# Sums of weights all formed in the second batch, seven products per block from the third batch on

## The chip, the core and the metric

The kernel runs on one core of a Trainium2 chip. The metric is the device time of one execution in microseconds (us), the median of several executions. The engines are named as in the profile: PE is TensorE (matmuls), PEld its weight loads, DVE is VectorE, ACT is ScalarE, POOL is GpSimd, SP is SyncE, which here issues transfers only.

## The reference

There are eight batches. In each, attention with eight heads (576 positions, head size 64, a window of 128 earlier positions, a linear bias by distance) gives 576 rows of 512 numbers. They then go through a bilinear feed-forward layer.

```python
scores = scale * np.matmul(q, k.transpose(0, 1, 3, 2))
mask = (rel >= 0) & (rel < window)
scores = np.where(mask, scores + bias[None], -1000000000.0)
attn = softmax(scores)                      # written out in the reference
attn_out = np.matmul(attn, v)
x = attn_out.transpose(0, 2, 1, 3).reshape(B * S, H * D)      # 4608 x 512
a, b = x @ w_a, x @ w_b                                       # 512 x 1536 each
return (a * b) @ w_out                                        # 1536 x 512
```

## The kernel before

All numbers are kept as pairs of 16-bit halves (a high part and a rest), so one product of two matrices takes three matmuls: high by high, high by rest, rest by high. The 1536 hidden columns are cut into 12 blocks `f`, the 576 rows of a batch into two halves of 288, the 512 inputs into chunks of 128.

**Stages.** PE's order is written out by hand: `batch(b)` weaves the feed-forward work of batch b with the attention of later batches, which `Pace` spreads evenly over it. So each batch has an *up* stage (both first products of the layer, all 12 blocks) and a *down* stage (the last product, tiles `dn_ps`, L952), and between these matmuls stand the attention's: scores `sc_ps` (L384), row norms `qtot` (L337), probabilities times values `x_ps` (L507). I call the stages by batch: the second batch is the first that `batch` handles (b = 1); the first batch has its own functions.

**Two ways for a block.** `up_plain` computes the four quarter results of a block (two row halves by a and b) as eight half products, 48 matmuls of 128x128 by 128x288. `up_fast` gets them from seven (Winograd's scheme), 42 matmuls, and needs sums: of the inputs (further slots of `xs`, made in `split_x` from the attention's output, some of them by POOL at L455, L458, L460, L465), and of the weights (`wsum`, and slot 3 of `wup` written over). In `up_fast` four of the seven products pass through one tile `ch` in turn, and ACT, DVE and POOL read and combine them as they come (L881 to L916). `ways[b]` says which blocks of batch b go which way: the second batch is all plain, the third has six plain blocks and six fast ones, the fourth two and ten, and from the fifth on all are fast.

**Steps that form sums of weights.** `sums_of_weights` has 24 steps, two for each block. A step is five POOL operations (L248 on 128x512, L249 to L252 on 128x128), and one step later two ACT copies (L258) and two DVE subtractions (L260) that split the sums into halves. The 16 steps of blocks 0 to 7 keep their interim sums in a part of `wsum` that is not yet in use; those of blocks 8 to 11 (`ws`) take two buffers each of the pool `t`, whose four buffers also hold the attention's exponentials. `quota[b]` says how many steps run beside the up stage and the down stage of batch b, and between which of its pieces: an entry `(a, z, steps)`. A twenty-fifth call only finishes the last step.

**What sets the other engines' order.** For ACT, DVE and POOL a scheduler puts the instructions of this program in the order in which its own clock has them ready, with some marked urgent; on the chip each engine then takes them strictly in that order. `issue_after` holds an instruction behind another in that clock.

Of the kernel before, what the change touches and what calls it, by code (L numbers as in the profile page):

```python
# [21 lines left out]
B, H, S, D = 8, 8, 576, 64  # L22
# [24 lines left out]
def attention_then_bilinear_ffn(ctx: ExitStack, tc: tile.TileContext, qT, kT, vP, w_a, w_b, w_out, rel, slopes2, outT):  # L47
# [221 lines left out]
    def load_v(b):  # L269

        st = State()
        st.v = work.tile([P, NPAIR, VCOLS], F32, tag="v", name="v")
        sp.dma_start(st.v, vP[b])
        st.xq = work.tile([P, S], BF16, tag="xq", name="xq")
        return st
# [93 lines left out]
    def scores(o, bi):  # L369

        ps = ps_at.tile([P, 512], F32, tag="at", name="sc_ps")
        t = work.tile([P, 512], F32, tag="t", name="t", bufs=4)
        for i, c in BANKS[bi]:
            w = TILES[i][1]
            qq, kk = slice(64 * i, 64 * i + 64), slice(64 * i + 64 - w, 64 * i + 64)
            if o.b == 1:
                with tc.issue_after(last_pv[0].ins):
                    for e in range(2):
                        r = slice(64 * e, 64 * e + 64)
                        pe.matmul(ps[r, c:c + w], o.q[r, qq], o.k[r, kk], start=True, stop=True)  # L380
                continue
            for ks, last in ((o.kh, False), (o.kl, True)):
                for e in range(2):
                    pe.matmul(ps[64 * e:64 * e + 64, c:c + w], o.qs[:, e, qq], ks[:, e, kk], start=not last, stop=last)  # L384
        for i, c in BANKS[bi]:
            pc, w = TILES[i]
            n = o.n
            vec.tensor_tensor_reduce(out=t[:, c:c + w], in0=ps[:, c:c + w], in1=o.bias[:, WIN - w:WIN], scale=-0.125 if o.b == 1 else o.neg, scalar=3.0e38, op0=ALU.add, op1=ALU.min, accum_out=o.mn[:, n:n + 1])  # L388
            act.activation(t[:, c:c + w], t[:, c:c + w], AF.Exp, bias=o.mn[:, n:n + 1], scale=-1.0, accum_out=o.sm[:, n:n + 1])  # L389
            o.parts.append((n, t[:, c:c + w], pc, w))  # L390
            o.n += 1
# [48 lines left out]
    def split(n, src):  # L440
        act.copy(xs[:, n, 0, :, :], src)  # L441
        vec.tensor_tensor(out=xs[:, n, 1, :, :], in0=src, in1=xs[:, n, 0, :, :], op=ALU.subtract)  # L442

    def split_x(st, plain, fast):

        b11, b12, b21, b22 = (st.v[:, k:k + 2, t:t + HT] for k in (0, 2) for t in (0, HT))
        split(0, b11)
        if plain:
            split(1, b21)
            split(2, b22)  # L450
            split(B12, b12)
        if not fast:
            return
        yield
        pool.tensor_tensor(out=b11, in0=b12, in1=b11, op=ALU.subtract)  # L455
        if not plain:
            split(2, b22)
        pool.tensor_tensor(out=b12, in0=b22, in1=b12, op=ALU.subtract)  # L458
        split(4, b11)
        pool.tensor_tensor(out=b22, in0=b22, in1=b11, op=ALU.subtract)  # L460
        yield
        if not plain:
            split(1, b21)
        split(6, b12)
        pool.tensor_tensor(out=b21, in0=b21, in1=b22, op=ALU.subtract)  # L465
        yield
        split(5, b22)
        split(3, b21)
        yield
# [197 lines left out]
    def attention():  # L667
# [16 lines left out]
        def split(o):  # L684
            if o and o.b > 1:
                split_qk(o)
# [10 lines left out]
        st, prev = load_v(1), None  # L697
# [4 lines left out]
        for i in range(n + 1):  # L702
            b, p = 1 + i // NPAIR, i % NPAIR

            two = 2 if o and o.b >= 2 else 1
            for bi in range(two if o else 0):
                scores(o, bi)
            with behind():
                nxt = squares(i + 1)
            if p == 1 and b > 1:  # L710
                st = load_v(b)
            if p == (1 if b == 1 else 2):
                v_scale(st)
            yield i + 1 / 7
            if o and two == 1:
                scores(o, 1)

            if p == 2:

                with tc.issue_after(first_reads[0].ins) if first_reads[0] else ExitStack():  # L720
                    late.vhl = split_v(st, late.p)
            elif prev and p != 1:
                prev.vhl = split_v(st, prev.p)
            yield i + 2 / 7
            if p == 2:
                pv(late.p, st, late, late.vhl)
                transpose_probs(prev)
                split(nxt)
            if o and p != 2:
                with behind():  # L730
                    normalize(o)
            if p != 2:
                split(nxt)
            yield i + 3 / 7
            if o:
                scores(o, 2)
            if prev and p not in (1, 2):
                pv(prev.p, st, prev, prev.vhl)
            if two == 2 and p in (1, 3):
                if p == 2:  # L740
                    with behind():
                        normalize(o)
                scores(o, 3)
            yield i + 4 / 7
            if p == 2:
                prev.vhl = split_v(st, prev.p)
                if two == 1 or p not in (1, 3):
                    with behind():
                        normalize(o)
            if o and (two == 1 or p not in (1, 3)):  # L750
                scores(o, 3)
            lay_out(nxt)
            load(i + 2)
            if p == (0 if b == 1 else 1):
                v_squares(st, (0, 1))
            if prev and p == 0:
                states[b - 1] = st
                assert started["down"] == b - 2
                for k, _ in enumerate(split_x(st, b - 1 <= 3, b - 1 >= 2)):
                    yield i + (4.2 + 0.2 * k) / 7  # L760
            yield i + 5 / 7
            if o:
                with behind():
                    normalize(o)
            if p == (0 if b == 1 else 1):
                v_squares(st, (2, 3))
            yield i + 6 / 7
            if prev and p == 0:
                hidden_scale(st)
            if p == 2:  # L770
                pv(prev.p, st, prev, prev.vhl)
            if p == 1:
                late = prev
            elif o:
                transpose_probs(o)
            prev, o = o, nxt
            yield i + 1
# [232 lines left out]


    every = list(range(NF))
    ways = [(every, [])] * 2 + [(every[6:], every[:6]), (every[10:], every[:10])] + [([], every)] * (B - 4)
    att = Pace(attention())
    spread = sums_of_weights()

    quota = [((), ()), (((8, 48, 9),), ((0, 48, 4),)), (((0, 24, 3),), ((0, 48, 5),)), ((), ((0, 48, 4),))] + [((), ())] * (B - 4)

    def first_batch():
        st = states[0]  # L1020
# [60 lines left out]
```

## Time and profile before

| | |
|---|---|
| Time, median of 3 executions | 991.28 us (991.03 to 994.67) |
| The profiled execution | 989.81 us, span of its instructions 988.0 us |
| PE, DVE, ACT, POOL busy in the span | 962.1, 669.0, 635.6, 255.3 us |
| Matmuls | 9339 in the record |
| Second batch | up 200.3 to 281.8 us, down to 324.1 |
| Third batch | up to 400.0 us, down to 441.1 |
| Fourth batch | up to 513.2 us, down to 554.8 |

The stage bounds are where PE's first matmul of the next kind starts (L952 for down, L856 for up). All times are from the start of the span. A row of the trace's timeline reads: start, duration, engine, line, operation, output <- inputs, shape, count, and in brackets the idle time of that engine just before, with what ended it.

### The profile page before, as it was taken

What the parts mean: (1) busy time and instruction counts of PE and PEld (TensorE: products, weight loads), DVE (VectorE), ACT (ScalarE), POOL (GpSimd) and SP (SyncE); (2) the same over time, 40 slices, a digit from 0 to 9 for tenths busy, and PEclk for the clock granted to TensorE, in tenths of its full rate; (3) what the DMA queues carried; (4) which work ended last, traced back from release to release, by engine and by line L of the source; (5) the groups of instructions that cost most, each with busy time, mean ns of one, the idle gap of its engine ahead of it and who ended that gap; (6) DMA issues with size and microseconds to landing.
All of it is one profiled execution on the core that took longest, in us unless ns stands there. A gap on an engine that the chain in (4) does not pass through costs nothing.

```text
span 988.0 us, 23867 instructions
## 1 busy us (share of the span) xinstructions
PE 962.1 (97%) x9339; PEld 748.9 (76%) x9339; DVE 669.0 (68%) x1867; ACT 635.6 (64%) x1729; POOL 255.3 (26%) x309
## 2 busy tenths in 40 slices
PE   7899999999999999999999999999999999999998
PEld 5567777677777777777777777777777777877776
DVE  5979998668688657777778677757776576514520
ACT  5977769667676667766767766777667766413321
POOL 1211122032546313541225222211232012311100
PEclk8999999999999999999999999999999999999999
DMA  8434753664337234463345362373245432200001
GB/s 333 168 126 172 231 154 67 151 158 92 80 74 183 68 69 87 107 172 75 68 92 121 120 118 65 87 191 84 59 84 117 133 74 38 55 34 5 1 13 36
DMA packets 148432, 102.82 MB, mean 104 GB/s; under 512 B 120032, under 2 KB 128352, under 8 KB 147296
## 3 DMA queue, kind: packets, MB, share of 16 engines
q1 hardware_dynamic: 138816, 91.77, 38.2%
q10 hardware_dynamic: 9504, 9.54, 3.0%
q8 instruction: 73, 1.20, 0.5%
q14 instruction: 39, 0.32, 0.1%
HBM read 48.33 MB, written 9.44 MB: 58 GB/s over the span
## 4 chain that ended last, share of the span: by engine, by line
PE 69%; DVE 12%; ACT 7%; DMA 7%; issue 3%; POOL 1%; SPq 0%; ACTq 0%; DVEq 0%
PE ch L856 19%; PE dn_ps L952 18%; PE p L856 14%; PE up_ps L856 9%; PE x_ps L507 4%; DMA v<-in_vP 4%; PE sc_ps L384 3%; DVE phl L406 2%; PE dn_ps L818 2%; ACT t L389 1%; DVE wsum L135 1%; DVE xs L442 1%; ACT phl L405 1%; DVE wsum L134 1%; DMA qk<-in_kT 1%
## 5 line engine op out<-in xcount | busy, mean ns | idle before, releaser
L856 PEld LDWEIGHTS <-wup 128*128 128x128 f16 x3072 | 296.3, 98 | 82.0 <-issue 5.7
L952 PE MATMUL dn_ps<-h,wdn 128*128 128x288 f16 x2016 | 254.4, 286 | 0.0
L952 PEld LDWEIGHTS <-wdn 128*128 128x128 f16 x2016 | 193.9, 98 | 52.0 <-issue 0.2
L856 PE MATMUL up_ps<-xs,wup 128*128 128x288 f16 x1536 | 194.6, 286 | 1.1 <-ACT rc L867 0.8
L856 PEld LDWEIGHTS <-wsum 128*128 128x128 f16 x1152 | 111.7, 98 | 32.0 <-issue 2.5
L911 POOL TENSOR_TENSOR rc<-rc,row 128x288 f32<-128x288 f32 x64 | 62.3, 974 | 279.8 <-DVE row L909 263.9
L389 ACT ACTIVATE t<-t,mn 128x192 f32<-128x192 f32 (+2 forms) x252 | 107.2, 427 | 24.5 <-DVE mn L388 24.4
L856 PE MATMUL ch<-xs,wup 128*128 128x288 f16 x768 | 115.0, 286 | 0.5 <-ACT row L893 0.5
L856 PE MATMUL p<-xs,wup 128*128 128x288 f16 x768 | 115.1, 286 | 0.0
L406 DVE SCALAR_TENSOR_TENSOR phl<-t,rin,phl 128x192 f16<-128x192 f32 (+2 forms) x252 | 104.6, 454 | 15.3 <-ACT phl L405 15.1
L856 PE MATMUL ch<-xs,wsum 128*128 128x288 f16 x768 | 111.5, 286 | 1.1 <-ACT rc L881 1.1
L848 ACT CAST h<-rc 128x576 f16<-128x576 f32 x96 | 64.1, 668 | 69.1 <-DVE rc L916 37.2
L405 ACT ACTIVATE phl<-t,rin 128x192 f16<-128x192 f32 (+2 forms) x252 | 88.9, 425 | 25.3 <-DMA pT<-phl 12.7
L849 DVE TENSOR_TENSOR h<-rc,h 128x576 f16<-128x576 f32 x90 | 69.5, 772 | 30.5 <-ACT h L848 29.7
L388 DVE CUSTOM_DVE_ANT_0 t<-sc_ps,bias,neg 128x192 f32<-128x192 f32 (+2 forms) x216 | 73.9, 389 | 7.6 <-PE sc_ps L384 7.5
L957 ACT ACTIVATE row<-dn_ps,oi 128x288 f32<-128x288 f32 x56 | 27.6, 493 | 55.9 <-PE dn_ps L952 55.9
L893 ACT ACTIVATE row<-ch,g 128x288 f32<-128x288 f32 x64 | 31.8, 497 | 48.9 <-PE ch L856 48.9
L442 DVE TENSOR_TENSOR xs<-v,xs 128x576 f16<-128x576 f32 x52 | 47.8, 935 | 21.4 <-ACT xs L441 21.3
L888 DVE TENSOR_TENSOR rc<-p,rc 128x288 f32<-128x288 f32 x64 | 29.1, 454 | 44.3 <-PE p L856 34.7
L365 POOL TENSOR_SCALAR bias<-rel_sb,ninv,sl_sb 128x192 f32<-128x192 f32 x24 | 20.0, 832 | 147.8 <-DVE mn L388 129.8
L856 PE MATMUL p<-xs,wsum 128*128 128x288 f16 x384 | 57.5, 286 | 0.0
L436 POOL TENSOR_TENSOR xq<-xq,sq 128x576 bf16<-128x576 bf16 x22 | 29.2, 1325 | 75.7 <-ACT sq L435 75.7
(155 smaller groups left out, 1386.1 us busy)
## 6 DMA issues: line engine op xcount, KB each, us to landing
v<-in_vP SPq DMA_DIRECT2D x8, 1280.0 KB, 6.2
out<-row ACTq DMA_DIRECT2D x62, 144.0 KB, 1.8
qk<-in_qT SPq DMA_DIRECT2D x28, 288.0 KB, 4.0
qk<-in_kT SPq DMA_DIRECT2D x28, 288.0 KB, 4.4
wdn<-in_w_a SPq DMA_DIRECT2D x12, 512.0 KB, 5.1
wdn<-in_w_b SPq DMA_DIRECT2D x12, 512.0 KB, 6.1
wdn<-in_w_out SPq DMA_DIRECT2D x12, 512.0 KB, 4.6
qst<-qkh SPq DMA_DIRECT2D x24, 144.0 KB, 2.7
```

The source lines that it names most:

```text
L388: vec.tensor_tensor_reduce(out=t[:, c:c + w], in0=ps[:, c:c + w], in1=o.bias[:, WIN - w:WIN], scale=-0.125 if o.b == 1 else o.neg, scalar= ...
L389: act.activation(t[:, c:c + w], t[:, c:c + w], AF.Exp, bias=o.mn[:, n:n + 1], scale=-1.0, accum_out=o.sm[:, n:n + 1])
L405: act.activation(phl[:, 0, pc:pc + w], e, AF.Copy, scale=s)
L406: vec.scalar_tensor_tensor(out=phl[:, 1, pc:pc + w], in0=e, scalar=s, in1=phl[:, 0, pc:pc + w], op0=ALU.mult, op1=ALU.subtract)
L442: vec.tensor_tensor(out=xs[:, n, 1, :, :], in0=src, in1=xs[:, n, 0, :, :], op=ALU.subtract)
L507: last = pe.matmul(xp[oc // 512][64 * h:64 * h + 64, o0:o0 + w], vt[0:rows, c:c + 64], probs(pt, rows, blocks, h), start=(n == 0 and first ...
L848: act.copy(h[:, f, :, 0, :], hid)
L849: eng.tensor_tensor(out=h[:, f, :, 1, :], in0=hid, in1=h[:, f, :, 0, :], op=ALU.subtract)
L856: pe.matmul(ps[:, 0:HT], w[:, wi, k, :], xs[:, b, xi, k, :], start=(first and n == 0), stop=(last and n == len(ks) - 1), skip_group_check= ...
L893: last_read[0] = last_main[0] = act.activation(mid, ch, AF.Copy, scale=st.g)
L911: pool.tensor_tensor(out=x0, in0=x0, in1=mid, op=ALU.mult)
L952: pe.matmul(ps[:, 0:HT], wdn[:, f, wi, e * P:(e + 1) * P], h[:, f, t, hi, :], start=(m == 0 and n == 0), stop=(m == NF - 1 and n == 2))
```

## The change

Two tables and one condition change. All 24 steps (and the finishing call) run in the second batch, 15 beside its up stage and 10 beside its down stage; before, it was 13 there, 8 in the third batch, 4 in the fourth. The third and fourth batch use `up_fast` for all 12 blocks. And `split_x` no longer makes slot B12 of `xs` for these two, so it makes seven splits (L441 on ACT, L442 on DVE) in place of eight, in the order that the fifth batch already has.

```diff
-                for k, _ in enumerate(split_x(st, b - 1 <= 3, b - 1 >= 2)):
+                for k, _ in enumerate(split_x(st, b - 1 <= 1, b - 1 >= 2)):
...
-    ways = [(every, [])] * 2 + [(every[6:], every[:6]), (every[10:], every[:10])] + [([], every)] * (B - 4)
+    ways = [(every, [])] * 2 + [([], every)] * (B - 2)
...
-    quota = [((), ()), (((8, 48, 9),), ((0, 48, 4),)), (((0, 24, 3),), ((0, 48, 5),)), ((), ((0, 48, 4),))] + [((), ())] * (B - 4)
+    quota = [((), ()), (((4, 48, 15),), ((0, 48, 10),))] + [((), ())] * (B - 2)
```

PE's order is the same as before in every stage but the up stages of the third and fourth batch, and these two now read row for row like that of the fifth. There 36 and 12 matmuls go. On the other engines the order changes from the second batch's up stage on.

POOL at the end of the second batch's up stage, up to the first sum of inputs for the third (L455). Before:

```order
L252 TENSOR_TENSOR wsum<-wsum 128x128
L249 TENSOR_TENSOR wsum<-wsum 128x128
L252 TENSOR_TENSOR wsum<-wsum 128x128
L250 TENSOR_TENSOR wsum<-wsum 128x128
L251 TENSOR_TENSOR wsum<-wsum 128x128
L252 TENSOR_TENSOR wsum<-wsum 128x128
L455 TENSOR_TENSOR v<-v 128x2x288
L458 TENSOR_TENSOR v<-v 128x2x288
L436 TENSOR_TENSOR xq<-xq,sq 128x576
L365 TENSOR_SCALAR bias<-rel_sb,ninv,sl_sb 128x192
L248 TENSOR_TENSOR wsum<-wup 128x512 x2
L460 TENSOR_TENSOR v<-v 128x2x288
```

Now, at the same place:

```order
L249 TENSOR_TENSOR wsum<-wsum 128x128
L252 TENSOR_TENSOR wsum<-wsum 128x128
L248 TENSOR_TENSOR wsum<-wup 128x512
L250 TENSOR_TENSOR wsum<-wsum 128x128
L251 TENSOR_TENSOR wsum<-wsum 128x128
L249 TENSOR_TENSOR wsum<-wsum 128x128
L252 TENSOR_TENSOR wsum<-wsum 128x128
L250 TENSOR_TENSOR wsum<-wsum 128x128
L251 TENSOR_TENSOR wsum<-wsum 128x128
L455 TENSOR_TENSOR v<-v 128x2x288
L252 TENSOR_TENSOR wsum<-wsum 128x128
L248 TENSOR_TENSOR ws_4275<-wup 128x512
```

Since the last bias (L365) POOL now has four steps instead of three ahead of L455, all but the fourth's L252, and behind it come steps of the last four blocks.

ACT at the same place, where the split of that sum (the last L441 here) stands ahead of the last hidden block's copy (L848). Before:

```order
L867 COPY rc<-up_ps 128x288
L258 CAST wup<-wsum 128x128
L258 CAST wsum<-wsum 128x3x128
L441 CAST xs<-v 128x576 x2
L848 CAST h<-rc 128x2x288
L389 ACTIVATE t,sm<-t,mn 128x64
```

Now:

```order
L867 COPY rc<-up_ps 128x288
L258 CAST wup<-wsum 128x128
L258 CAST wsum<-wsum 128x3x128
L258 CAST wup<-wsum 128x128
L258 CAST wsum<-wsum 128x3x128
L441 CAST xs<-v 128x576
L848 CAST h<-rc 128x2x288
L389 ACTIVATE t,sm<-t,mn 128x64
```

One more pair of copies stands in front, and the split that waits for L455 is still ahead of L848.

DVE in the second half of that batch's down stage, around `both` (L329), for which PE's `qtot` waits. Before:

```order
L388 ISA t,mn<-sc_ps,bias,neg 128x192
L388 ISA mn 128x1
L329 TENSOR_SCALAR both<-halves,qs 128x2
L442 TENSOR_TENSOR xs<-v,xs 128x576
L402 RECIPROCAL rin<-rin 128x5
```

Now:

```order
L442 TENSOR_TENSOR xs<-v,xs 128x576
L964 TENSOR_SCALAR oi<-g,smin,so 128x1
L965 TENSOR_SCALAR oi<-oi,sv 128x1
L966 RECIPROCAL oi<-oi 128x1
L329 TENSOR_SCALAR both<-halves,qs 128x2
L260 TENSOR_TENSOR wup<-ws_4488,wup 128x128
L260 TENSOR_TENSOR wsum<-ws_4424,wsum 128x3x128
L388 ISA t,mn<-sc_ps,bias,neg 128x64
```

`both` has moved ahead of the scores' operations (L388), and between it and them stand subtractions of the steps.

## The prediction

> **What bounds the kernel now.** I read the page first: busy times, granted clock, and the chain that ended last.
>
> ```profile
> PE 962.1 (97%) x9339; PEld 748.9 (76%) x9339; DVE 669.0 (68%) x1867; ACT 635.6 (64%) x1729; POOL 255.3 (26%) x309
> ...
> PEclk8999999999999999999999999999999999999999
> ...
> PE 69%; DVE 12%; ACT 7%; DMA 7%; issue 3%; POOL 1%; SPq 0%; ACTq 0%; DVEq 0%
> ```
>
> PE is busy 97% of the span at full clock, and the chain lies on it for 69%. So a matmul that goes is worth its time, and an operation elsewhere costs nothing until PE waits for it. Second view: busy time by stage, cut where PE goes from up to down and back. The rows are up and down of the second, third, fourth, fifth and sixth batch in turn.
>
> ```profile
> core 0: us, PE busy (x) PEld busy (x) DVE busy (x) ACT busy (x) POOL busy (x), PEclk, DMA share, GB/s
> 200.30:281.80 81.50, 80.25 (x799) 63.27 (x798) 61.10 (x176) 59.44 (x172) 38.11 (x56) 1.00 0.47 105
> 281.80:324.10 42.30, 41.13 (x409) 31.89 (x408) 33.18 (x98) 30.36 (x90) 20.74 (x23) 1.00 0.61 146
> 324.10:400.00 75.90, 74.96 (x747) 59.16 (x745) 52.54 (x144) 50.88 (x136) 18.57 (x25) 1.00 0.30 65
> 400.00:441.10 41.10, 40.86 (x408) 31.83 (x406) 30.98 (x96) 29.34 (x88) 21.32 (x27) 1.00 0.67 159
> 441.10:513.20 72.10, 71.89 (x723) 56.78 (x721) 52.17 (x146) 50.90 (x137) 17.57 (x19) 1.00 0.37 76
> 513.20:554.80 41.60, 40.87 (x409) 31.81 (x406) 30.58 (x96) 29.51 (x89) 19.04 (x22) 1.00 0.60 150
> 554.80:626.40 71.60, 71.14 (x711) 55.58 (x709) 52.58 (x149) 50.71 (x135) 16.31 (x16) 1.00 0.37 75
> 626.40:667.10 40.70, 40.70 (x408) 31.91 (x407) 25.45 (x93) 29.05 (x87) 8.72 (x7) 1.00 0.62 157
> 667.10:737.80 70.70, 70.70 (x710) 55.51 (x708) 50.78 (x144) 48.85 (x130) 16.32 (x16) 1.00 0.35 73
> 737.80:778.60 40.80, 40.80 (x409) 31.97 (x408) 24.56 (x90) 27.77 (x83) 8.71 (x7) 1.00 0.67 153
> ```
>
> The fifth and sixth batch are what the third and fourth are to become: all blocks by seven products, no steps beside them. DVE's column shows what the steps cost beside PE: in a down stage it is busy 33.2, 31.0 and 30.6 us with them, 25.5 and 24.6 without.
>
> **The gain.** 36 matmuls go from the third batch and 12 from the fourth. In a run of fast products, six matmuls follow the six before them in 0.74 us:
>
> ```profile
> 561.72 0.90 PE L856 MATMUL p<-xs,wup 128*128 128x288 f16 x6
> 562.46 0.90 PE L856 MATMUL ch<-xs,wsum 128*128 128x288 f16 x6
> ```
>
> So 48 of them are 48 x 0.74 / 6 = 5.9 us. By stages instead: PE's order there becomes that of the fifth batch, so I put the mean of the fifth and sixth in their place. Up: 71.15, against 75.90 and 72.10, saves 4.75 and 0.95. Down: 40.75, against 41.10 and 41.60, saves 0.35 and 0.85. Together 6.9 us, of which about 1.0 are waits that go with the steps. I take 6.9; the bounds are 5.9 (the waits stay) and 7.6 (5.9, and PE's whole idle time of the four stages, 2.1 us, falls to the 0.46 of the fifth and sixth batch's means). The split of slot B12 that both batches save (one L441, one L442 each) lies beside PE and counts nothing.
>
> **What the moved steps take.** Twelve calls move into the second batch: six more beside its up stage (9 to 15), six more beside its down stage (4 to 10, the last of which only finishes). One step, by the rows of the `ws` tiles:
>
> ```profile
> L248 POOL TENSOR_TENSOR ws<-wup x8: 1145/1152/1266, 402.2 to 545.8; 128x512 f32<-128x512 f16 x8
> ...
> L252 POOL TENSOR_TENSOR ws<-ws,ws x8: 453/457/652, 405.4 to 553.1; 128x128 f32<-128x128 f32 x8
> L258 ACT CAST wup<-ws x8: 283/286/298, 417.3 to 556.8; 128x128 f16<-128x128 f32 x8
> L258 ACT CAST wsum<-ws x8: 509/512/522, 417.5 to 557.0; 128x384 f16<-128x384 f32 x8
> L260 DVE TENSOR_TENSOR wup<-ws,wup x8: 279/292/743, 417.6 to 557.1; 128x128 f16<-128x128 f32 x8
> L260 DVE TENSOR_TENSOR wsum<-ws,wsum x8: 545/558/1755, 418.2 to 557.5; 128x384 f16<-128x384 f32 x8
> ```
>
> POOL takes 1.15 + 4 x 0.457 = 2.98 us, ACT 0.80, DVE 0.85. DVE's part is dearer than that while POOL works. These are DVE's groups of the second batch's down stage (four steps' subtractions), then one of the fifth's (none):
>
> ```profile
> L406 DVE SCALAR_TENSOR_TENSOR phl<-t,rin,phl 128x192 f16<-128x192 f32 x10 | 6.6, 701 | 0.5 <-ACT phl L405 0.5
> L260 DVE TENSOR_TENSOR wsum<-wsum 128x384 f16<-128x384 f32 x4 | 4.2, 1044 | 0.0
> L260 DVE TENSOR_TENSOR wup<-wsum,wup 128x128 f16<-128x128 f32 x4 | 3.2, 807 | 1.0 <-ACT wup L258 1.0
> L406 DVE SCALAR_TENSOR_TENSOR phl<-t,rin,phl 128x192 f16<-128x192 f32 x13 | 4.7, 413 | 0.6 <-ACT phl L405 0.6
> ```
>
> The same L406 takes 701 ns beside POOL's steps and 413 without; the two L260 take 1.85 us there, not 0.85. So a step costs DVE 0.85 to 1.85 us. The Trainium skill states the reason (SBUF — State Buffer, Who interferes with whom): a VectorE instruction with two SBUF inputs and a GpSimd instruction that reads SBUF exclude each other for the whole instruction, whichever issues first. The trace agrees that they delay each other, by 0.29 us for an L406 on average; how far the exclusion goes decides the second rival.
>
> **What it costs, place by place in the second batch.** PE's order is unchanged there, so each cost is a wait of PE.
>
> *Up stage.* ACT goes from 59.4 to 59.4 + 6 x 0.80 = 64.2 of 81.5 us, DVE from 61.1 to 66 to 72. PE idles 1.25 us there now (81.50 less 80.25) with nine steps; six more in proportion add 0.8. Bounds: 0, since five banks stand between a product and its copy, and 2.5, twice the present idle time.
>
> *The last hidden block.* POOL has a fourth step to do ahead of L455. Now the chain there is this:
>
> ```profile
> 281.76 1.40 POOL L455 TENSOR_TENSOR v<-v 128x576 f32<-128x576 f32 x1 [0.69 <-DVE xs L442]
> 283.19 0.67 ACT L441 CAST xs<-v 128x576 f16<-128x576 f32 x1 [1.04 <-POOL v L455]
> 284.23 0.67 ACT L848 CAST h<-rc 128x576 f16<-128x576 f32 x1 [0.37 <-DVE rc L869]
> 286.27 0.75 DVE L849 TENSOR_TENSOR h<-rc,h 128x576 f16<-128x576 f32 x1
> 283.47 4.75 PE L952 MATMUL dn_ps<-h,wdn 128*128 128x288 f16 x36
> ```
>
> ACT waits for L455, and behind that split stands L848, the copy of block 11 of `h`; DVE's L849 completes it at 287.0. PE goes through the blocks in order, three matmuls each; it comes back from a set of scores at 283.47 with six or seven of them done, and is at block 11 after some 27 more of 0.123 us, at 286.8. So there is no slack. The fourth step puts 1.15 + 3 x 0.457 = 2.5 us in front of L455; 1.4 us of it are free, as L849 starts that much after L848 ends (DVE works on scores), so 1.1 remain, and DVE's own extra pair in front is 0.85 to 1.85 more, partly in the same time. I take 1.7 us; bounds 0 (POOL gets its fourth step done earlier) and 3.
>
> *`qtot`.* The only wait for another engine over 0.15 us that the list of waits gives for this down stage is
>
> ```profile
> PE qtot L337 <- DVE both L329: 1.2, 1, 1.2
> ```
>
> `both` moves ahead of five scores' operations of DVE, and POOL has one L248 and two quarter-size operations less between L458 and L465. ACT's copy ahead of `both` should be done sooner. I take 0.6 us gained; bounds 1.2 gained and 1.5 lost (POOL behind by what the last paragraph adds).
>
> *Rest of the down stage.* DVE's L388, which free the banks of `sc_ps`, now stand behind subtractions that wait for ACT, and these for POOL. DVE goes from 33.2 to 33.2 + 4 x (0.85 to 1.85) = 36.6 to 40.6 of 42.3 us, POOL to 8.72 + 8 x 2.98 = 32.6. I take 0.5 us; bounds 0 and 2.
>
> *Start of the third batch's up stage.* It is fast from its first block, and `ch` must be read before PE can go on. The steps' ends stand in front: POOL's last two steps follow the bias, which starts only when the scores before it are done, and ACT and DVE have one step left over. Two rows show how tight that place is: POOL's wait for those scores in the second batch, and PE's wait in the fifth, behind the end of a step.
>
> ```profile
> 319.03 0.50 POOL L365 TENSOR_SCALAR bias<-rel_sb,ninv,sl_sb 128x192 f32<-128x192 f32 x1 [8.94 <-DVE mn L388]
> 557.85 0.90 PE L856 MATMUL ch<-xs,wsum 128*128 128x288 f16 x6 [0.42 <-ACT rc L881]
> ```
>
> If the bias comes 2 to 3 us later than 319.0, two steps of 2.98 end at 327 to 328, 3 to 4 us into the stage, where the fifth waits for such a copy already. I take 1.2 us, three times the 0.42; bounds 0 and 4.
>
> Sum: 0.8 + 1.7 - 0.6 + 0.5 + 1.2 = 3.6 us given back, of 6.9. The profiled execution took 989.81 us (span 988.0, 1.8 around it), 1.5 below the median of 991.28; the difference of -3.3 us is put on both: span 984.7, median **988.0 us**. After the fourth batch nothing changes.
>
> **The rivals.**
>
> *All of the cost is hidden.* For it: DVE and ACT come to 96% at most in the sums above, and the third and fourth batch pay only 0.24 and 0.73 us of PE's idle time in down stages with five and four calls. Against it: the chain to L849 has no slack. Less than 1.9 us given back, about 1.0: 991.28 - 6.9 + 1.0 = 985.4.
>
> *Slower: VectorE and GpSimd exclude each other and bound the down stage.* If no two-input operation of DVE can run beside one of POOL, their times add in the second batch's down stage: POOL 32.6 us; DVE 10 x 0.413 of L406, 8 x 0.85 of L260, and some six splits at 0.75 to 0.99 (5.8 us by the fifth batch's group), 16.7 together. That is 49.3 in a stage of 42.3, so 7.0 us come on top of the 3.6: 991.28 - 6.9 + 10.6 = 995.0. It decides from where the two together exceed the stage. For it: 701 against 413 ns. Against it: that is a delay of 0.29 us an operation, and an operation that has waited can run while POOL starts its next. The Trainium skill's rule, taken strictly, is this rival.
>
> *It does not do what it says.* The third batch's fast blocks wait for sums of weights, and the 4.75 us of its up stage don't come. Blocks are taken in order, though, and those of the last steps are wanted last, some 60 us later. 6.9 - 4.75 - 3.6 = -1.45: 992.7.
>
> **How the numbers follow.** A measurement of this kernel tells about 0.5% (5 us) from no change, so faster means under 986.3 and slower over 996.2. Part of the gain given back (986.3 to 991): 0.57, and this is the forecast; its own range is 986.3 to 990.8. All hidden: 0.26. VectorE and GpSimd bound: 0.12, about half of it above 996.2. Sums come late: 0.05. Faster 0.28 (the hidden case and a little of the first), slower 0.06, same 0.66. The range 985.0 to 993.0 takes in the late sums and some of the slower rival; it leaves out the rest of that (0.1) and the best third of the hidden case (0.09).
>
> **What would show it.** Third batch's up stage at 71 to 73 us (4 lost at most at its start) and the fourth's at 71; their down stages at 40.7; the second batch's up and down at 82 and 44 instead of 81.5 and 42.3; PE waiting for `h` (L849) some 5 us into that down stage, with POOL's L455 at 284 or later; the wait for `both` smaller. Wrong would be: no such wait for `h`; a down stage of 47 us or more, with DVE busy throughout and L406 near 1 us; or a third batch whose `ch` products wait for L258 or L260.

## The result, and the profile after

The changed kernel takes **998.04 us** (median of 6 runs, 996.59 to 999.11), the kernel before 992.03 in runs beside it (6 runs, 988.85 to 994.67). The ratio is 1.0061, with a 95% interval of 1.0040 to 1.0082: slower by 6 us, where 3.3 us less were forecast and 993.0 was the upper end. The profiled execution took 998.96 us, its span is 997.1.

Page of the changed kernel, busy times of the engines:

```profile
PE 962.9 (97%) x9291; PEld 747.4 (75%) x9291; DVE 675.6 (68%) x1881; ACT 638.7 (64%) x1735; POOL 269.1 (27%) x317
```

The 48 matmuls have gone (9291, before 9339), and yet PE is as long busy as before (962.9 and 962.1 us). Busy time by stage of the changed kernel, columns as in the prediction; up and down of the second, third and fourth batch in turn:

```profile
203.40:287.80 84.40, 80.54 (x800) 63.38 (x798) 69.03 (x184) 62.48 (x181) 57.96 (x81) 1.00 0.44 98
287.80:333.90 46.10, 41.33 (x408) 31.77 (x406) 40.46 (x104) 31.44 (x91) 33.41 (x41) 1.00 0.55 130
333.90:409.80 75.90, 72.44 (x710) 56.12 (x709) 56.00 (x156) 53.75 (x147) 23.43 (x27) 0.98 0.35 72
409.80:450.50 40.70, 40.70 (x408) 31.91 (x406) 24.29 (x88) 27.16 (x82) 8.73 (x7) 1.00 0.61 153
450.50:523.10 72.60, 71.17 (x711) 55.60 (x710) 52.02 (x148) 50.81 (x136) 16.32 (x16) 1.00 0.35 74
523.10:563.80 40.70, 40.70 (x409) 31.91 (x407) 25.46 (x93) 28.99 (x87) 8.72 (x7) 1.00 0.62 157
```

The second batch has become 2.9 us longer in its up stage (81.5 before) and 3.8 in its down stage (42.3). The third batch's up stage has the length it had before, 75.9 us, with 36 matmuls less. DVE is busy 8 us longer beside the second batch's up stage and 7 beside its down stage. In the first batch, whose order did not change, the down stage took 48.5 us against 46.8; it also takes 48.4 in the fastest kernel below, so that is not the change. From the second to the fourth batch the two profiles differ by 5.9 us.

The list of what PE waited for, from the second batch's up stage to the start of the third's (in total, times, longest), without its last lines:

```profile
PE sc_ps L384 <- DVE mn L388: 3.5, 2, 2.6
PE ch L856 <- ACT rc L881: 3.1, 1, 3.1
PE dn_ps L952 <- DVE h L849: 2.8, 1, 2.8
...
PE qtot L337 <- DVE both L329: 0.6, 1, 0.6
PE dn_ps L952 <- ACT h L848: 0.4, 1, 0.4
...
```

Before, the same list had the wait of 1.2 us for `both` that the prediction shows, and no more than these two:

```profile
PE up_ps L856 <- ACT rc L867: 0.8, 1, 0.8
PE sc_ps L384 <- DVE mn L388: 0.4, 1, 0.4
```

Three places carry it: scores in the up stage (2.6), the last block of `h` (2.8 + 0.4), and the first `ch` of the third batch (3.1). Rows of the timeline at the second of them, picked from all engines:

```profile
290.24 1.72 POOL L455 TENSOR_TENSOR v<-v 128x576 f32<-128x576 f32 x1
290.62 1.49 DVE L260 TENSOR_TENSOR wup<-wsum,wup 128x128 f16<-128x128 f32 x1
291.99 0.67 ACT L441 CAST xs<-v 128x576 f16<-128x576 f32 x1 [2.56 <-POOL v L455]
292.38 1.15 POOL L248 TENSOR_TENSOR ws<-wup 128x512 f32<-128x512 f16 x1
292.45 1.49 DVE L260 TENSOR_TENSOR wsum<-wsum 128x384 f16<-128x384 f32 x1
292.57 0.67 ACT L848 CAST h<-rc 128x576 f16<-128x576 f32 x1
295.61 0.75 DVE L849 TENSOR_TENSOR h<-rc,h 128x576 f16<-128x576 f32 x1
296.41 0.77 PE L952 MATMUL dn_ps<-h,wdn 128*128 128x288 f16 x5 [2.84 <-DVE h L849]
```

The chain is the forecast one: ACT stands 2.56 us behind L455, L848 behind that split. L849, which completes the block, begins 2.4 us after L848 has ended (292.57 + 0.67 = 293.24). Now look at DVE's two L260: 1.49 us each, where they take 0.28 and 0.55 alone. The first begins inside L455, which ends at 291.96, and ends 0.15 us after it; the second begins inside L248, which ends at 293.53, and ends 0.41 after it. At the third place (some of ACT's rows, then PE's, then the clock while it was low):

```profile
336.85 0.30 ACT L258 CAST wup<-ws 128x128 f16<-128x128 f32 x1 [0.56 <-POOL ws L249]
337.06 1.49 ACT L405 ACTIVATE phl<-t,rin 128x192 f16<-128x192 f32 x4
338.45 0.50 ACT L258 CAST wsum<-ws 128x384 f16<-128x384 f32 x1
339.25 0.38 ACT L881 COPY rc<-ch 128x288 f32<-128x288 f32 x1
...
339.68 1.60 PE L856 MATMUL ch<-xs,wsum 128*128 128x288 f16 x6 [3.11 <-ACT rc L881]
341.07 1.55 PE L856 MATMUL p<-xs,wsum 128*128 128x288 f16 x6
...
338.97:342.39 3.42, 2.71 (x12) 1.69 (x12) 3.42 (x13) 2.94 (x10) 2.66 (x5) 0.50 0.13 46
```

ACT reaches the copy of `ch` only at 339.25, behind the copies of a step and the probabilities of the last scores. PE waits 3.11 us, and then finds the granted clock at 0.50 for 3.42 us: two sets of six matmuls start 1.39 us apart instead of 0.74, which costs another 1.3 us.

### The profile page after: what moved, and what is told of

The parts are those of the page before. It is cut to its first block, busy times and chain, and to the rows that moved or that the text cites. A ratio compares the mean times of both kernels' runs of the same rounds, so it can differ in the third digit from the quotient of the medians.

```text
span 997.1 us, 23816 instructions
## 1 busy us (share of the span) xinstructions
PE 962.9 (97%) x9291; PEld 747.4 (75%) x9291; DVE 675.6 (68%) x1881; ACT 638.7 (64%) x1735; POOL 269.1 (27%) x317
## 4 chain that ended last, share of the span: by engine, by line
PE 63%; DVE 13%; DMA 9%; ACT 8%; issue 4%; POOL 3%; SPq 0%; ACTq 0%; DVEq 0%; POOLq 0%
PE ch L856 21%; PE dn_ps L952 16%; PE p L856 15%; PE x_ps L507 4%; DMA v<-in_vP 4%; PE sc_ps L384 3%; PE dn_ps L818 2%; ACT t L389 2%; DVE phl L406 2%; DMA pT<-phl 2%; DVE wsum L135 1%; DVE t L388 1%; DVE wsum L134 1%; ACT phl L405 1%; DMA wdn<-in_w_b 1%
## 5 line engine op out<-in xcount | busy, mean ns | idle before, releaser
L856 PEld LDWEIGHTS <-wup 128*128 128x128 f16 x2880 | 277.5, 98 | 78.9 <-issue 7.2
L911 POOL TENSOR_TENSOR rc<-rc,row 128x288 f32<-128x288 f32 x72 | 69.9, 970 | 319.5 <-DVE row L909 302.4
L856 PEld LDWEIGHTS <-wsum 128*128 128x128 f16 x1296 | 126.4, 98 | 39.5 <-issue 5.8
L856 PE MATMUL up_ps<-xs,wup 128*128 128x288 f16 x1152 | 146.4, 286 | 0.6 <-ACT rc L867 0.3
L856 PE MATMUL ch<-xs,wup 128*128 128x288 f16 x864 | 129.4, 286 | 1.4 <-ACT row L893 1.3
L856 PE MATMUL ch<-xs,wsum 128*128 128x288 f16 x864 | 126.4, 287 | 4.3 <-ACT rc L881 4.3
L856 PE MATMUL p<-xs,wup 128*128 128x288 f16 x864 | 129.5, 286 | 0.0
L406 DVE SCALAR_TENSOR_TENSOR phl<-t,rin,phl 128x192 f16<-128x192 f32 (+2 forms) x252 | 100.9, 441 | 15.4 <-ACT phl L405 15.1
L405 ACT ACTIVATE phl<-t,rin 128x192 f16<-128x192 f32 (+2 forms) x252 | 88.7, 425 | 25.9 <-DMA pT<-phl 13.7
L848 ACT CAST h<-rc 128x576 f16<-128x576 f32 x96 | 64.1, 667 | 62.2 <-DVE rc L916 37.7
L849 DVE TENSOR_TENSOR h<-rc,h 128x576 f16<-128x576 f32 x90 | 70.9, 787 | 25.8 <-ACT h L848 25.0
L893 ACT ACTIVATE row<-ch,g 128x288 f32<-128x288 f32 x72 | 35.9, 499 | 64.0 <-PE ch L856 64.0
L388 DVE CUSTOM_DVE_ANT_0 t<-sc_ps,bias,neg 128x192 f32<-128x192 f32 (+2 forms) x216 | 74.1, 389 | 2.8 <-PE sc_ps L384 2.7
L856 PE MATMUL p<-xs,wsum 128*128 128x288 f16 x432 | 65.4, 288 | 0.0
L442 DVE TENSOR_TENSOR xs<-v,xs 128x576 f16<-128x576 f32 x50 | 47.5, 964 | 24.3 <-ACT xs L441 24.1
L365 POOL TENSOR_SCALAR bias<-rel_sb,ninv,sl_sb 128x192 f32<-128x192 f32 x24 | 20.5, 853 | 131.4 <-DVE mn L388 124.2
L916 DVE SCALAR_TENSOR_TENSOR rc<-rc,g,ch 128x288 f32<-128x288 f32 x72 | 36.7, 510 | 24.9 <-PE ch L856 24.9
```

Source lines behind the costliest of these rows:

```text
L405: act.activation(phl[:, 0, pc:pc + w], e, AF.Copy, scale=s)
L406: vec.scalar_tensor_tensor(out=phl[:, 1, pc:pc + w], in0=e, scalar=s, in1=phl[:, 0, pc:pc + w], op0=ALU.mult, op1=ALU.subtract)
L848: act.copy(h[:, f, :, 0, :], hid)
L849: eng.tensor_tensor(out=h[:, f, :, 1, :], in0=hid, in1=h[:, f, :, 0, :], op=ALU.subtract)
L856: pe.matmul(ps[:, 0:HT], w[:, wi, k, :], xs[:, b, xi, k, :], start=(first and n == 0), stop=(last and n == len(ks) - 1), skip_group_check= ...
L911: pool.tensor_tensor(out=x0, in0=x0, in1=mid, op=ALU.mult)
```

## The experiments

Stage lengths, cut as above, and the median time of each kernel; the kernel before had medians of 991.0 to 992.0 us beside them. Where a kernel ran once, "one" stands behind its time. The stage lengths are of one profiled execution each. That one can lie some us from the median (1003.7 us for early_end), and the second batch begins at 199.7 to 206.3 us in the 13 profiles, so the stages say where time went better than a single time does.

| kernel | us | second up | second down | third up |
|---|---|---|---|---|
| before | 991.3 | 81.5 | 42.3 | 75.9 |
| changed | 998.0 | 84.4 | 46.1 | 75.9 |
| steps_alone | 1002.0 | 84.1 | 49.0 | 77.2 |
| blocks_alone | 983.7 | 80.8 | 41.6 | 71.2 |
| pool_part | 991.6 | 84.3 | 43.1 | 75.0 |
| copy_part | 990.8 | 84.3 | 40.7 | 73.6 |
| up_copies | 988.2 one | 81.1 | 43.1 | 76.1 |
| up_pool | 990.3 one | 80.8 | 43.9 | 75.9 |
| early_end | 997.3 | 84.2 | 47.3 | 78.2 |
| into_third | 995.8 | 81.1 | 41.6 | 81.4 |
| no_reads | 988.8 | 83.6 | 41.1 | 73.5 |
| third_no_reads | 990.0 one | 82.1 | 40.7 | 75.4 |
| spread_out | 994.6 | 80.7 | 42.2 | 79.8 |

### The two parts of the change apart

*steps_alone*: the changed quota, with the ways of the kernel before.

```diff
-    ways = [(every, [])] * 2 + [([], every)] * (B - 2)
+    ways = [(every, [])] * 2 + [(every[6:], every[:6]), (every[10:], every[:10])] + [([], every)] * (B - 4)
```

> All 24 steps in the second batch as in the change, but the third and fourth batch by the blocks of before (so plain blocks there read a slot of wup that already holds sums, which leaves their numbers wrong and their work the same). Theory of the queues: what was lost is PE's waits for ACT, DVE and POOL in the second batch, so its up stage is some 84 us and its down stage some 46, as after the change, the third batch's up stage starts without the 3 us wait (plain first), and the time is 997 to 998 us against 992 before. Rival, the fast stages don't gain: the second batch alone costs nothing, and the time is about 991.

*blocks_alone*: the changed ways, 13 calls of steps in the second batch as before, the other steps left out.

```diff
-    quota = [((), ()), (((4, 48, 15),), ((0, 48, 10),))] + [((), ())] * (B - 2)
+    quota = [((), ()), (((8, 48, 9),), ((0, 48, 4),))] + [((), ())] * (B - 2)
...
+        f = block % 6
```

> All blocks fast from the third batch on as in the change, but the steps only up to the thirteenth call, as the second batch has them before; the later ones are left out, and the fast blocks 6 to 11 read the weight sums of blocks 0 to 5. Theory of the queues: the full 6.9 us are gained, up stages of 71 us in the third and fourth batch, down stages of 40.7, the second batch at 81.5 and 42.3; time 985. Rival, the fast stages don't gain: up stages of 74 to 76 us there, time 990 to 992.

Measured: blocks_alone 983.65 us, ratio 0.9923 (0.9901 to 0.9945), so the fast blocks, with no steps beside them, are worth 7.6 us; steps_alone 1001.97, ratio 1.0113 (1.0094 to 1.0132), so moving the steps cost 10.7 there. The gain came out near the forecast; the cost did not. steps_alone is also 4 us over what was expected of it: its down stage has a wait of 4.2 us for `h` and half clock for 6.83 us from there on. In blocks_alone the third batch's up stage has the forecast length and PE hardly idles in it:

```profile
202.30:283.10 80.80, 80.24 (x799) 63.28 (x798) 60.83 (x174) 58.82 (x169) 38.09 (x56) 1.00 0.46 104
283.10:324.70 41.60, 40.95 (x408) 31.89 (x407) 32.24 (x97) 30.19 (x90) 19.27 (x22) 1.00 0.62 147
324.70:395.90 71.20, 71.12 (x711) 55.56 (x709) 52.33 (x148) 50.53 (x135) 16.31 (x16) 1.00 0.36 76
```

Against it the twelve moved calls cost the changed kernel 14.4 us: 3.6, 4.5 and 4.7 us in these three stages. Most of the rest, 1.1 us, lies ahead of the second batch, where nothing was changed.

### POOL's half of a step, and the half of ACT and DVE

*pool_part*: the last twelve steps do only their five POOL operations. *copy_part*: they do only their copies and subtractions, from a buffer that is ready.

```diff
+                if 2 * g + m >= 12:                 # pool_part: no copies and subtractions
+                    yield
+                    continue
...
+                z = whole                           # copy_part: POOL's operations only in the first twelve
+                if 2 * f + k < 12:
```

> The changed kernel, but of the twelve moved steps only POOL's five operations; their copies on ACT and subtractions on DVE are left out (fast blocks 6 to 11 read the sums of blocks 0 to 5). If POOL's work, through the exclusion of DVE and through its own lateness, is what costs, the time is 995 to 998; if the moved work of ACT and DVE is, 986 to 988. I expect something between, 991.

> The changed kernel, but of the twelve moved steps only the copies on ACT and subtractions on DVE, from a buffer that lies ready; POOL's five operations are left out. If POOL's work is what costs, 986 to 988; if the work of ACT and DVE is, 995 to 998. I expect 988, with the wait for the last hidden block gone, since POOL has nothing ahead of L455.

Measured: 991.6 (ratio 1.0008, 0.9992 to 1.0025) and 990.8 (0.9996, 0.9979 to 1.0012). Each half alone costs 7 to 8 us over blocks_alone, both 14.4. That looks like a sum, but the table says otherwise: in the up stage both halves show the whole loss (84.3), since the twelve steps ahead of the wait for scores are whole in both kernels. In the down stage, where they do differ, the copies alone cost nothing (40.7), POOL's operations 1.5 us, both 4.5. So the two interact. copy_part lost the wait for `h`, as expected of it, and yet came out above the 988 us expected: the up stage kept its loss, and the start of the third batch a wait of 1.8 us.

*up_copies* and *up_pool* do the same to the steps beside the up stage.

```diff
+                if 2 * f + k > 14:                  # up_copies: POOL's operations only behind the up stage
...
+                if g is not None and 2 * g + m < 14:  # up_pool: copies and subtractions only behind it
+                    yield
+                    continue
```

> The fifteen steps beside the second batch's up stage do without their five POOL operations (ACT and DVE split a ready buffer of zeros instead); the steps of the down stage are whole, and the fast blocks use the sums of blocks 8 to 11. DVE's order stays. First theory, POOL's operations lengthen DVE's there (L849 and five L406 took 1.70 and 2.54 us at 262 us, against 0.93 and 1.52 in the kernel with the fast blocks alone): the wait of 2.6 us for scores at 272 us falls to about 0.4 to 0.8, up stage 81.5 to 82.5 us; L455 also finds POOL free, and the wait for h of 2.8 us falls below 1. Second theory, the copies and subtractions themselves are in the way: the wait of 2.6 us stays, up stage 84 us.

> The opposite: the first fourteen steps keep POOL's operations beside the second batch's up stage, and their two copies on ACT and two subtractions on DVE are left out; the fast blocks use the sums of blocks 8 to 11. First theory (POOL lengthens DVE): the wait for scores at 272 us stays at 1.5 to 2.6 us, up stage 83 to 84.4 us, and h comes late still, by 1.5 to 2.8 us. Second theory (copies and subtractions): the wait falls to about 0.4 us, up stage 81.5 us, and h is on time.

Each theory was right for its own kernel, and neither for the cause: **either** half left out brings the up stage back to 81 us, and only both together make 84.4. In both kernels the wait for scores is 0.64 us instead of 2.59. DVE's rows ahead of the scores at 272.6 us say why. First of the changed kernel, then of blocks_alone, at the same place of the program:

```profile
261.86 1.70 DVE L849 TENSOR_TENSOR h<-rc,h 128x576 f16<-128x576 f32 x1 [0.49 <-ACT h L848]
263.49 2.54 DVE L406 SCALAR_TENSOR_TENSOR phl<-t,rin,phl 128x64 f16<-128x64 f32 x5
272.60 0.27 PE L384 MATMUL sc_ps<-qkh,qst 128*64 128x192 f16 x2 [2.59 <-DVE mn L388]
```

```profile
258.99 0.93 DVE L849 TENSOR_TENSOR h<-rc,h 128x576 f16<-128x576 f32 x1 [0.49 <-ACT h L848]
259.85 1.52 DVE L406 SCALAR_TENSOR_TENSOR phl<-t,rin,phl 128x64 f16<-128x64 f32 x5
268.00 0.27 PE L384 MATMUL sc_ps<-qkh,qst 128*64 128x192 f16 x2 [0.41 <-DVE mn L388]
```

Beside POOL's steps these six operations take 4.2 us instead of 2.5. DVE also comes to this stretch 0.7 us later, measured against PE, and one more L260 (0.28 us) stands in it; some of DVE's idle time goes in return, and PE waits 2.2 us more. In up_pool the five L406 still take 2.55 us, but no subtractions stand beside them and DVE has idle time to spare; in up_copies they take 1.53.

### Is it the place?

*early_end* lets the last three calls run in the third batch's up stage, so that no step ends at its start. *into_third* keeps the second batch as before and runs twelve calls beside the third batch's up stage.

```diff
-    quota = [((), ()), (((4, 48, 15),), ((0, 48, 10),))] + [((), ())] * (B - 2)
+    quota = [((), ()), (((4, 48, 15),), ((0, 34, 7),)), (((8, 32, 3),), ())] + [((), ())] * (B - 3)      # early_end
+    quota = [((), ()), (((8, 48, 9),), ((0, 48, 4),)), (((0, 66, 12),), ())] + [((), ())] * (B - 3)      # into_third
```

> The changed kernel, but its last three calls of steps run in the third batch's up stage, some 7 us apart from its eighth piece on, and the seven calls before them within the first 34 pieces of the second batch's down stage. No copy of a step then stands on ACT ahead of the first copy of ch. First theory, the start of the third batch is a queue on ACT and DVE behind the steps' ends, and the half clock follows from PE's wait: third batch up 71 to 72.5 us instead of 75.9, second batch up 84.3 and down 46 us as in the changed kernel, sum 993 to 995 us. Second theory, the work is what costs, not where it ends: third batch up stays at 75 to 76 us or the down stage grows by as much, sum 997 to 999 us.

> All 24 steps and all fast blocks of the changed kernel, but only the 13 calls that ran there before run in the second batch; the other 12 run beside the third batch's up stage, one for every 5.5 of its pieces (4.7 us). First theory, waits at three crowded places of the second batch (the scores at 272.6 us, the last block of h, the first ch product): these places are as in the kernel with the fast blocks alone, so second batch up 81 and down 41.5 us, third batch up 72 to 75 instead of 71.2 us, sum 985 to 988 us. Second theory, each moved step costs PE about 1.2 us wherever it runs (14.4 us for twelve): third batch up 80 us or more, sum 995 to 998 us.

My theory of three crowded places failed. early_end took 997.29 us (ratio 1.0061, 1.0040 to 1.0082): the wait of 3.1 us for the copy of `ch` fell to 1.3, and others took its place (1.9 for L916, 1.8 for L893, 1.5 for a DMA); the down stage was another 1.2 us longer, with half clock for 6.83 us from the wait for `h` on. into_third took 995.79 (1.0044, 1.0027 to 1.0060): the second batch was as in blocks_alone, and the third batch's up stage grew by 10.2 us. The list of its waits there, and the longest one in the timeline:

```profile
PE ch L856 <- DVE rc L916: 7.1, 4, 2.3
...
356.63 1.23 POOL L248 TENSOR_TENSOR ws<-wup 128x512 f32<-128x512 f16 x1
356.77 1.50 DVE L260 TENSOR_TENSOR wsum<-ws,wsum 128x384 f16<-128x384 f32 x1
358.20 0.50 DVE L916 SCALAR_TENSOR_TENSOR rc<-rc,g,ch 128x288 f32<-128x288 f32 x1
358.75 0.90 PE L856 MATMUL ch<-xs,wup 128*128 128x288 f16 x6 [2.26 <-DVE rc L916]
```

Again an L260 of 1.50 us that begins inside a POOL operation and ends 0.41 us after it (356.63 + 1.23 = 357.86; 356.77 + 1.50 = 358.27); behind it stands L916, the last reader of `ch`. The wait was where such operations meet, not at three places.

### The exclusion by itself

In the changed kernel's second down stage POOL and DVE can be watched taking turns (POOL's rows, then DVE's):

```profile
313.53 1.40 POOL L465 TENSOR_TENSOR v<-v 128x576 f32<-128x576 f32 x1
314.89 1.26 POOL L248 TENSOR_TENSOR ws<-wup 128x512 f32<-128x512 f16 x1
316.12 0.97 POOL L251 TENSOR_TENSOR ws<-ws,ws 128x128 f32<-128x128 f32 x1
...
313.91 1.23 DVE L406 SCALAR_TENSOR_TENSOR phl<-t,rin,phl 128x192 f16<-128x192 f32 x1
315.07 1.70 DVE L442 TENSOR_TENSOR xs<-v,xs 128x576 f16<-128x576 f32 x1
```

L465 ends at 314.93, L406 0.21 us after it. L248 ends at 316.15, L442 0.62 after it, at 316.77; and L251, which takes 0.46 us alone, ends 0.32 after that, at 317.09. Over the whole trace an L442 (0.75 us alone) that begins while a TENSOR_TENSOR of POOL is under way ends 0.61 to 0.62 us after that, whether it began 0.1 or 0.9 us into it (21 cases). A step's 128x128 operation that begins inside an L406 or L442 ends 0.31 to 0.34 us after it (26 of 27; the other began 0.01 us into it and went first). DVE's operations with one input from PSUM (L916, L909, L869, L388) keep their times. POOL's TENSOR_SCALAR does not take turns in this way: the bias L365 that begins at 307.92 us takes 1.99 us instead of 0.50, and two L442 in a row end ahead of it.

*no_reads* replaces a step's five POOL operations by six memsets of about the same total length, which only write. *third_no_reads* does this to into_third.

```diff
-                    pool.tensor_tensor(out=a, in0=wup[:, f, 0:4, 0, k, :], in1=wup[:, f, 0:4, 1, k, :], op=ALU.add)
...
+                    pool.memset(a, 0.0)
+                pool.memset(a, 0.0)
+                for n in (0, 0, 1, 1):
+                    pool.memset(z[:, n:n + 3, :], 0.0)
```

> The changed kernel, but each step's five POOL operations are replaced by six that only write (memsets of the same buffers, about 2 x 0.55 + 4 x 0.44 = 2.9 us by the three memset rows of the profile, against 2.98), so the sums are zeros; ACT's copies and DVE's subtractions stay, and DVE's order in the second batch's up stage is nearly the same. Theory now: a DVE operation with two inputs from SBUF cannot run while a POOL operation reads SBUF (L442 ends 0.61 us after such an operation of POOL, whenever it began), and that makes DVE late. Then the second batch's up stage falls from 84.4 to 81 to 82 us with POOL as busy as before, the wait of 2.6 us goes, L406 and L260 keep their undisturbed times, the down stage comes to 43 to 45 us (L455 still waits for the fourth step), sum 989 to 993 us. Rival: what costs is the length of the chain POOL, ACT, DVE and the queues behind it, whatever POOL does meanwhile: up 84, down 46, sum 996 to 999 us.

> The kernel with twelve calls beside the third batch's up stage, with the same replacement: POOL's operations of the steps only write, and the sums are zeros. Theory (two-input operations of DVE are shut out while POOL reads SBUF): third batch up falls from 81.4 us to 72.5 to 75 us, without the 7 us of waits for the product of L916. Rival (queues and DVE's own 0.85 us for each step): it stays at 79 to 82 us.

Measured: no_reads 988.8 us (ratio 0.9971, 0.9953 to 0.9989), third_no_reads 989.97 in one run. The second batch's stages of no_reads and the third's up stage:

```profile
205.40:289.00 83.60, 80.46 (x800) 63.34 (x798) 62.54 (x190) 62.83 (x185) 40.58 (x89) 1.00 0.48 105
289.00:330.10 41.10, 40.84 (x407) 31.81 (x406) 33.58 (x103) 31.27 (x93) 27.64 (x50) 1.00 0.55 131
330.10:403.60 73.50, 71.32 (x711) 55.65 (x709) 53.78 (x153) 52.86 (x143) 19.01 (x22) 1.00 0.37 80
```

DVE's group of the 128x192 operation from 200 to 420 us, of the changed kernel (mean 600 ns):

```profile
L406 DVE SCALAR_TENSOR_TENSOR phl<-t,rin,phl 128x192 f16<-128x192 f32 x52 | 29.2, 600 | 1.0 <-ACT phl L405 1.0
```

The same of no_reads, where the line is L405 (mean 460 ns):

```profile
L405 DVE SCALAR_TENSOR_TENSOR phl<-t,rin,phl 128x192 f16<-128x192 f32 x54 | 22.8, 460 | 1.3 <-ACT phl L404 1.3
```

POOL's other operations still read there. The 16 of these operations in the whole trace that meet memsets only take 0.40 to 0.42 us, as alone, and the six such splits (L441 in no_reads) 0.74 to 0.75. PE's wait for scores was 2.6 us in the changed kernel, and its waits for the last reader of `ch` 7.1 us in into_third. The first line is the one wait in no_reads, the second the other in third_no_reads:

```profile
PE sc_ps L383 <- DVE mn L387: 0.7, 1, 0.7
...
PE ch L855 <- DVE rc L915: 2.7, 4, 0.9
```

The down stage loses 5.0 us of its 46.1, the third batch's start 2.4 of 75.9, and into_third's third up stage 6.0 of 81.4 (75.4, a little over the range). Only the second batch's up stage stayed long, 83.6 us, and that is in part the memsets themselves: at one place twelve run in a row, and DVE's small cast beside them takes 5.05 us (DVE's row, POOL's first and last, then PE's).

```profile
218.57 5.05 DVE L285 CAST vc<-vs 128x4 bf16<-128x4 f32 x1 [0.81 <-ACT vsq L281]
...
217.95 1.45 POOL L248 MEMSET wsum<- 128x512 f32 x3
...
222.15 1.46 POOL L249 MEMSET wsum<- 128x512 f32 x3
...
223.73 4.57 PE L855 MATMUL up_ps<-xs,wup 128*128 128x288 f16 x36 [1.77 <-DVE rin L401]
```

PE waits 1.8 us behind this; less that, the stage has 81.8. So of the 14.4 us that the steps cost the changed kernel, 9.2 went with POOL's reads, and an estimated 11.0 (9.2 and the 1.8) would have without the cast's delay. The rest is left to the copies, the subtractions and their queues; no run here divides it. A step's memsets took 2.7 us, its operations 2.98 undisturbed. POOL's records in the up stage are 17 us shorter (40.6 for 58.0), and some 11 of these are what the steps' operations took over 2.98 us a step, beside DVE. In the up stage DVE's order is that of the changed kernel but for two subtractions. At the place of the wait for scores L849 and five L406 (L848 and L405 in no_reads) take 0.76 and 1.53 us, so that wait went with the reads. In the down stage 16 of DVE's 103 instructions stand elsewhere, and there a part of the 5.0 us may be the order's.

### A version in between

*spread_out* has eight fast blocks in the third batch, twelve in the fourth, and no more than five calls beside a stage after the second batch.

```diff
-    ways = [(every, [])] * 2 + [(every[6:], every[:6]), (every[10:], every[:10])] + [([], every)] * (B - 4)
+    ways = [(every, [])] * 2 + [(every[8:], every[:8])] + [([], every)] * (B - 3)
...
+    quota = [((), ()), (((8, 48, 9),), ((0, 48, 4),)), (((0, 60, 5),), ((0, 48, 4),)), (((0, 60, 3),), ())] + [((), ())] * (B - 4)
```

> A version between the two kernels, complete: 13 calls in the second batch as before, 5 beside the third batch's up stage, 4 beside its down stage, 3 beside the fourth's up stage; the third batch has eight fast blocks (sixteen steps are done by then), the fourth twelve. 24 matmuls go (3.0 us). Theory: what a step costs PE grows with how crowded its stage is, and these stages hold one step in 12 us or more in the up stages: third batch up 74.4 to 75.5 us, down 41, fourth batch up 71.2 to 72, down 40.7, sum 987 to 990 us. Rival: beside fast blocks each step costs the 0.85 us that twelve of them cost there: two more in the third batch's up stage and three in the fourth's give 4 us back, sum 991 to 993 us.

It took 994.64 us (ratio 1.0040, 1.0028 to 1.0053), worse than both expectations: 79.8 us in the third batch's up stage, with PE waiting for L916 again (2.1 us) and a stretch at half clock (the stage's granted clock is 0.98). Beside fast blocks even five steps cost more than the two further fast blocks bring. No complete version that ran beats the kernel before.

## Why the prediction was wrong

**The gain was nearly right, in part by luck.** 6.9 us were forecast (5.9 to 7.6), and blocks_alone measured 7.6. The third batch's up stage is 71.2 us there, against 71.15 forecast; the down stages are 40.7 and 40.8, against 40.75. But the fourth batch's up stage stayed at 72.3, where 71.15 were forecast, so the two batches gained 5.7 us by their stages. Another 1.4 came in the second batch (80.8 and 41.6 us), where no block changed; it was not forecast, and no run here explains it.

**The costs were mis-sized, each at the place named.** In the second batch's up stage 0.8 (0 to 2.5) was taken from its idle time "in proportion"; it was 2.9. There PE's wait for scores grew from 0.4 to 2.6 us. The last hidden block, 1.7 (0 to 3), was 3.2, by the chain described; the 1.4 us taken as free between L848 and L849 were not, since L849 began 2.4 us behind. `qtot` was right in size: the wait for `both` went from 1.2 to 0.6 us. It is 0.65 in blocks_alone too, where `both` stands as before, so the reason given for it is not shown. The rest of the down stage, 0.5, was 0.9 (a wait for scores). The start of the third batch, 1.2 (0 to 4), was 3.1 and 0.4 us of waits and 1.3 of half clock, which the forecast did not have. The fourth batch's up stage was 72.6 instead of 71.15, from waits at its start; blocks_alone has 72.3 there, so that is a gain that failed to come and not the steps. All of it together is 12.6 us, where 3.6 had been taken; 6.9 less 12.6 makes 5.7 us slower, and 6.0 were measured.

**The step that failed** is the reason given against the second rival: "that is a delay of 0.29 us an operation, and an operation that has waited can run while POOL starts its next". The rows show the opposite of its second half: POOL's next TENSOR_TENSOR waits for the one that has waited. The two engines alternate, one operation each, and a mean delay of 0.29 us over all L406 hides one of 0.2 to 1.1 for each that meets POOL. The Trainium skill (SBUF — State Buffer, Who interferes with whom) says that the one that issues first has the shared ports for its whole instruction; the trace agrees, with L442's 0.61 to 0.62 us behind every such end. The exclusion that the rival took was right, and 0.12 was too little for it. Its figure of 995.0 came near by other steps than the run took. It added the two engines' times in the down stage (49.3 us) with all eight steps of the last four blocks, of which two began only in the third batch (L248 at 335.13 and 338.26 us); the stage took 46.1, and PE lost its time there in single waits, not at the sum of two engines' work. The up stage and the third batch's start, where the engines exclude each other too, were left out. The same section says that a POOL instruction that only writes does not contend with the two-input kind, as no_reads shows.

**What a step costs was taken as its own durations.** 0.85 to 1.85 us of DVE a step counted its own pair. It did not count what POOL's 2.98 us do to the operations of the attention and of `h` that they meet: L849 at 1.70 instead of 0.93, five L406 at 2.54 instead of 1.52. That was to be seen in the rows quoted, since the 701 ns of L406 is such a delay; it was priced for L260 alone.

What stays open: how the 3.4 us that no_reads still has over blocks_alone (5.1, the 1.8 behind the cast set aside) divide between ACT, DVE and their queues.

## What to carry to other kernels

Before work is moved to an idle GpSimd, count VectorE's operations with two inputs from SBUF in that stage: each that meets a GpSimd operation that reads SBUF waits for its end, and the next such GpSimd operation for it (here GpSimd's TENSOR_TENSOR). Read it from ends, not from means: an operation that always ends the same time after another engine's end is shut out by it. And an engine's slack is spent once; either half of the added work was free in the up stage, and both together cost 3.6 us.

## What the runs showed of the hardware beyond that

PE's clock fell to half for 3.41 us after waits of 3.11 us (changed kernel) and 2.46 (pool_part) at the start of the third batch, and not after 1.81 (copy_part), nor after 3.11 in up_pool. After the wait of 2.84 us for `h` it did not in the changed kernel, and after the same wait in early_end it did, for 6.83 us. So the length of a wait alone does not decide it. The Trainium skill (TensorE: Matmul & The Clock Gate, Part 1) gives a window of 3413 ns that runs freely. The traces agree: in each of the 13, all changes of the granted clock lie whole multiples of 3.413 us apart (in the changed kernel 3.41, 34.13, 3.41, 150.19 and 3.41 us, from 147.83 us on). Lay this grid over PE's records from the second batch on. In the cell ahead of each fall to half clock PE stood idle for 2.10 to 3.00 us (seven falls, in seven kernels), and in every other cell at full clock for 1.89 at most. The wait of 2.84 us lay across two cells in the changed kernel, which had 1.45 and 1.81 us idle, and almost within one in early_end, which had 2.38. In the first batch 1.85 (steps_alone) and 1.83 us (no_reads) were enough, so idle time is not the whole rule.

And memsets, which leave two-input operations alone, shut out a cast of four elements a row that takes 0.17 us alone: for 5.05 us in no_reads, and for 2.26 and 2.86 in third_no_reads, each time until a run of memsets ended (0.02 us behind the last that it met). So another kind of VectorE operation is excluded by writes, and it does not take turns: in no_reads ten memsets that began after it went ahead of it.
